# Transposed local probabilities and pooled value products of the later batches write to the bank ring of the first matrix product

## Chip, cores and metric

One core of a Trainium2 chip runs the whole program. The metric is the device time of one execution in microseconds, the median of three runs. A profile of one more execution gives the rows that are shown here.

## What is computed

The reference chains an attention and two feed-forward stages, all in fp32:

```
q, k, v: (4 batches, 8 heads, 576 positions, 64)
out_d   = softmax(mean4(q) @ mean4(k).T / 8) @ mean4(v)      # pooled: 144 x 144 per head
local   = softmax(q @ k.T / 8 where |i - j| < 4) @ v         # a band of 7
x       = (repeat4(out_d) + local) as (2304 tokens, 512)
y       = leaky_relu(x @ w_in, 0.01) @ w_out                 # 512 -> 2048 -> 512
out     = (h - tanh(h)) @ w_out2,   h = y @ w_in2            # 512 -> 2048 -> 512
```

## The kernel before

**Tokens and blocks.** Each batch is cut into five units of 116 positions (the last one shorter), 20 units in all. Four units make a block of 460 or 464 tokens, so there are five blocks, and each feed-forward stage goes through all five: blocks 0 to 4 of the first stage, then five of the second.

**The feed-forward.** For a block, `f` counts 16 slices of the hidden layer, and one turn of that loop is called a step here. In a step `gemm1` (line 390) makes the hidden slice in a tile `hp` with 12 matmuls, ScalarE applies the activation (line 506 in the first stage) and rounds it to `gh` (line 511), VectorE makes the remainder `gl` (line 512), and `gemm2` (line 401) adds the slice of two steps ago to four accumulators with another 12 matmuls. Block 0 also converts the first stage's weights on the way (lines 333 to 353, ScalarE and VectorE), and its steps need those weights.

**The attention.** A local unit goes through three stages: scores (line 260) and their softmax; four transposes of the probabilities (line 287), copied out by ScalarE (line 289); the value product (line 301), added to the pooled result by VectorE (line 311). A pooled item (one pair of heads of one batch) also has three: scores (line 166) and softmax (lines 174 to 184); transposes (line 194), copied out at line 197; the value product (line 202), copied out at line 206. The units and pooled items of block 1 are computed while the feed-forward of block 0 runs, and so on. At the end of each step `advance()` emits the next stage of each item in flight, the oldest first; at most three are in flight.

**The order.** A scheduler that runs when the program is built puts the instructions on the engines by the order in which they were emitted and by when it expects their inputs; the engines then run their queues in that order. A tile that shares a tag with others takes one of the tag's buffers.

**PSUM.** Eight banks: four for the accumulators (`acc0`, `acc2`), two for `px`, two for the ring `h`. While the first batch's attention runs, before the feed-forward, the accumulator banks serve as `pe` tiles. After that (`early["on"]` is False) every attention product of the later units and batches takes the one `px` buffer of two banks:

```
ps_h = ctx.enter_context(tc.tile_pool(name="ps_h", bufs=2, space=bass.MemoryType.PSUM))
hp = ps_h.tile([128, 512], F32, tag="h", name="hp")          # gemm1, one for each f
p = banks()[:, 0]                                            # line 199, pooled value product
p = banks()[:, 0]                                            # line 284, transposed local probabilities
```

So the ring `h` holds nothing but `hp` tiles from the first step on, and `px` goes round through six kinds of product.

Of the kernel before, what the change touches and what calls it, by code (L numbers as in the profile page):

```python
# [7 lines left out]
F32 = mybir.dt.float32  # L8
# [56 lines left out]
def tile_attention_moe(  # L65
# [19 lines left out]
    ps_h = ctx.enter_context(tc.tile_pool(name="ps_h", bufs=2, space=bass.MemoryType.PSUM))  # L85
# [24 lines left out]
    early = {"on": True, "n": 0}  # L110

    def banks(first=False):
        if early["on"]:
            early["n"] += first
            tag = EARLY_S[early["n"] % len(EARLY_S)] if first else EARLY_T
            if tag != "px":
                return ps_a.tile([128, 2, 512], F32, tag=tag, name="pe")
        return ps_x.tile([128, 2, 512], F32, tag="px", name="px")

    nat = {}  # L120

    def load_first():
# [37 lines left out]
    def emit_down(b, c):  # L160
        qs, vs = pooled[b][0][:, c], pooled[b][1][:, c]
        ps = banks(True)
        for ii in range(2):
            for par in range(2):
                r = slice(par * D, (par + 1) * D)
                nc.tensor.matmul(  # L166
                    out=ps[:HD, par, ii * SD:(ii + 1) * SD], lhsT=qs[r, 0, ii * HD:(ii + 1) * HD],
                    rhs=qs[r, 1, :], start=True, stop=True,
                )
        nm = sb.tile([HD, 2, 2], F32, tag="nm", name="nm", bufs=3)  # L170
        sm = sb.tile([HD, 2, 2], F32, tag="sm", name="sm", bufs=3)
        pr = sb.tile([HD, 2, 2, SD], F32, tag="pr", name="pr", bufs=PRB)
        pv = ps[:HD, :, :2 * SD].rearrange("p b (a j) -> p b a j", a=2)
        nc.vector.tensor_reduce(nm, pv, AX.X, ALU.max)
        nc.vector.tensor_scalar(out=nm, in0=nm, scalar1=-SCALE / 16.0, scalar2=None, op0=ALU.mult)
        for par in range(2):
            for ii in range(2):
                nc.scalar.activation(  # L178
                    out=pr[:, par, ii, :], in_=pv[:, par, ii, :], func=ACTF.Exp,
                    bias=nm[:, par, ii:ii + 1], scale=SCALE / 16.0, accum_out=sm[:, par, ii:ii + 1],  # L180
                )
        nc.vector.tensor_scalar(out=sm, in0=sm, scalar1=1e-9, scalar2=4.0, op0=ALU.add, op1=ALU.mult)
        nc.vector.reciprocal(out=sm, in_=sm)
        nc.vector.tensor_tensor(
            out=pr, in0=pr, in1=sm.unsqueeze(3).to_broadcast([HD, 2, 2, SD]), op=ALU.mult
        )
        yield
        pt = sb.tile([HD, 2, 2, SD], F32, tag="pt", name="pt", bufs=PTB)
        p = banks()
        for par in range(2):  # L190
            for jj in range(2):
                for ii in range(2):
                    o = jj * SD + ii * HD
                    nc.tensor.transpose(  # L194
                        p[:HD, par, o:o + HD], pr[:, par, ii, jj * HD:(jj + 1) * HD], id_sb[:HD, :HD]
                    )
        nc.scalar.copy(out=pt, in_=p[:HD, :, :2 * SD].rearrange("p b (a j) -> p b a j", a=2))
        yield
        p = banks()[:, 0]
        for jj in range(2):  # L200
            for par in range(2):
                nc.tensor.matmul(  # L202
                    out=p[par * D:(par + 1) * D, :SD], lhsT=vs[:, jj, par, :], rhs=pt[:, par, jj, :],
                    start=(jj == 0), stop=(jj == 1),
                )
        nc.scalar.copy(out=outd[b][:, c, :], in_=p[:, :SD])
        if b == 0:
            yield
            n = BLOCKS[0][1]
            dst = xf[0][:, c, :n].rearrange("p (i r) -> p i r", r=4)  # L210
            up = outd[0][:, c, :n // 4].unsqueeze(2).to_broadcast([128, n // 4, 4])
            nc.vector.tensor_tensor(out=dst, in0=dst, in1=up, op=ALU.add)
            split_x(xf[0], split0(), c, n)
# [20 lines left out]
    def emit_unit(i):  # L234
        b, u, n = UNITS[i]
        j = i // BU
        off = b * S + u * QB - BLOCKS[j][0]
        if i not in loaded:
            load_unit(i)
        q, kt, v = loaded.pop(i)  # L240

        def operands(r, c, k):
            if q is not None:
                return q[r, c, k], kt[r, c, k]
            t = nat[(k % 2) * 2 + k // 2]
            w = (2 * u + c) * CB
            return t[r, 0, HALO + w:HALO + w + KB], t[r, 1, w:w + KB]

        kind = 0 if u == 0 else (2 if u == NU - 1 else 1)
        p = banks(True)  # L250
        pv = p[:, :, :NC * KB].rearrange("p h (k x) -> p h k x", x=KB)
        for h in range(2):
            r = slice(h * D, (h + 1) * D)
            if i < U_PE:
                edge = band_sb[:, kind].unsqueeze(1).to_broadcast([128, NC, KB])
                nc.tensor.matmul(out=p[:, h, :NC * KB], lhsT=id_bf, rhs=edge, start=True, stop=False)
            for k in range(NC):
                for c in range(2):
                    lhs, rhs = operands(r, c, k)
                    nc.tensor.matmul(  # L260
                        out=pv[c * KB:(c + 1) * KB, h, k], lhsT=lhs, rhs=rhs,
                        start=i >= U_PE, stop=i >= U_PE or k == NC - 1,
                    )
        nm = sb.tile([128, 2 * NC], F32, tag="lnm", name="lnm", bufs=4)
        sm = sb.tile([128, 2 * NC], F32, tag="lsm", name="lsm", bufs=4)
        pr = slot("lpr", i).rearrange("p (h k x) -> p h k x", h=2, k=NC)
        nmv, smv = (t.rearrange("p (h k) -> p h k", h=2) for t in (nm, sm))

        def each(t):
            return t.unsqueeze(3).to_broadcast([128, 2, NC, KB])  # L270

        if i >= U_PE:
            edge = band_f[:, kind].unsqueeze(1).unsqueeze(1).to_broadcast([128, 2, NC, KB])
            nc.vector.tensor_tensor(out=pr, in0=pv, in1=edge, op=ALU.add)
            pv = pr
        nc.vector.tensor_reduce(nmv, pv, AX.X, ALU.max)
        nc.vector.tensor_tensor(out=pr, in0=pv, in1=each(nmv), op=ALU.subtract)
        nc.scalar.activation(out=pr, in_=pr, func=ACTF.Exp, scale=SCALE)
        nc.vector.tensor_reduce(smv, pr, AX.X, ALU.add)
        nc.vector.tensor_scalar(out=sm, in0=sm, scalar1=1e-9, scalar2=None, op0=ALU.add)  # L280
        nc.vector.reciprocal(out=sm, in_=sm)
        nc.vector.tensor_tensor(out=pr, in0=pr, in1=each(smv), op=ALU.mult)
        yield
        p = banks()[:, 0]
        prt = pr.rearrange("p h (f g) x -> p (h f) (g x)", g=2)
        for t in range(NC):
            nc.tensor.transpose(p[:, t * 128:(t + 1) * 128], prt[:, t], id_sb)  # L287
        ptf = slot("lpt", i)
        nc.scalar.copy(out=ptf, in_=p)
        pt = ptf.rearrange("p (h f c x) -> p h f c x", c=2, f=2, h=2)  # L290
        if BU <= i + NLD < len(UNITS):
            load_unit(i + NLD)
        yield
        p = banks().rearrange("p g (f x) -> p (g f) x", f=2)
        for c in range(2):
            m = min(CB, n - c * CB)
            for g in range(2):
                r = slice(g * KB, (g + 1) * KB)
                for f in range(2):
                    for h in range(2):  # L300
                        nc.tensor.matmul(  # L301
                            out=p[h * D:(h + 1) * D, g * 2 + f, c * CB:c * CB + m],
                            lhsT=v[r, c, f, h], rhs=pt[r, h, f, c, :m], start=True, stop=True,
                        )
        if j not in xf:
            xf[j] = sb.tile([128, NC, NMAX], F32, tag="xf", name="xf")
        if i < BU:
            nc.scalar.copy(out=xf[j][:, :, off:off + n], in_=p[:, :, :n])
            return
        up = outd[b][:, :, u * QB // 4:(u * QB + n) // 4]  # L310
        nc.vector.tensor_tensor(
            out=xf[j][:, :, off:off + n].rearrange("p c (i r) -> p c i r", r=4),
            in0=p[:, :, :n].rearrange("p c (i r) -> p c i r", r=4),
            in1=up.unsqueeze(3).to_broadcast([128, NC, n // 4, 4]), op=ALU.add,
        )
# [295 lines left out]
```

## Time and profile before

| what | us |
|---|---|
| median of 3 runs | 939.44 (937.93 to 940.49) |
| the profiled execution | 937.61 |
| its span, first to last instruction | 935.7 |
| around the span | 1.9 |

The profile names an instruction by engine, line, operation and tiles (`hp<-xh,w` writes `hp` and reads `xh` and `w`). PE is TensorE's matmuls and PEld its weight loads, DVE is VectorE, ACT is ScalarE, POOL is GpSimd. PEclk is the share of TensorE's full clock that was granted. A matmul's end is modelled, and pipelined matmuls overlap: their starts are the safer reading.

### The profile page before, as it was taken

To read this page: it belongs to the slowest core of one execution; us is meant where nothing else is said; L and a number is where in the kernel's file an instruction comes from. 1 tells how busy PE (TensorE), PEld (TensorE's weight loads), DVE (VectorE), ACT (ScalarE), POOL (GpSimd) and SP (SyncE) were. 2 spreads that over 40 slices of the span, in tenths; PEclk is the share of its full clock that TensorE was granted. 3 is DMA by queue.
4 is the path that set the end of the run, shared out by engine and by line. 5 is a ranking of instruction groups with operands and counts; after the bars stand their busy time and mean duration, and the time that the engine had idled before them with its cause. 6 is when DMAs were issued, how large, how long until landed. Compare 5 with 4: busy or idle time off the path is not lost.

```text
span 935.7 us, 13925 instructions
## 1 busy us (share of the span) xinstructions
PE 915.6 (98%) x5790; PEld 796.0 (85%) x5790; DVE 432.3 (46%) x779; ACT 354.2 (38%) x731; POOL 46.0 (5%) x76
## 2 busy tenths in 40 slices
PE   7889999999999999999999999999999999999997
PEld 6777788788887888888888888888888988888896
DVE  6989994444244414512366878322232223223222
ACT  2666654342344233222454645232232233224221
POOL 1011130013000100000000000000000000000000
PEclk9979999999999999999999999999999999999999
DMA  9996362146010202000466800010020010001001
GB/s 318 393 263 205 70 131 96 35 105 151 11 64 23 71 11 86 25 0 7 168 222 203 279 5 1 20 61 1 1 81 1 1 59 22 1 1 41 1 1 40
DMA packets 25790, 76.58 MB, mean 82 GB/s; under 512 B 3200, under 2 KB 10624, under 8 KB 25728
## 3 DMA queue, kind: packets, MB, share of 16 engines
q1 hardware_dynamic: 19008, 52.50, 15.8%
q0 software_dynamic: 6720, 23.21, 10.0%
q8 instruction: 45, 0.74, 0.3%
q14 instruction: 17, 0.14, 0.0%
HBM read 66.26 MB, written 9.44 MB: 81 GB/s over the span
## 4 chain that ended last, share of the span: by engine, by line
PE 91%; DMA 3%; ACT 2%; DVE 2%; issue 1%; SPq 0%; ACTq 0%; DVEq 0%
PE hp L390 43%; PE acc L401 42%; PE px L260 2%; DMA qk<-qk 1%; DMA v<-vd 1%; PE px L301 1%; PE px L287 1%; PE px L202 1%; PE px L166 1%; DMA out<-ev 1%; PE px L194 1%; DMA x2d<-ev 0%; ACT wm L333 0%; ACT w L352 0%; ACT pr L178 0%
## 5 line engine op out<-in xcount | busy, mean ns | idle before, releaser
L390 PE MATMUL hp<-xh,w 128*128 128x460 f32 (+1 forms) x1280 | 379.9, 377 | 4.3 <-ACT xh L368 2.2
L401 PE MATMUL acc<-gh,w 128*128 128x460 f32 (+1 forms) x1280 | 373.0, 372 | 0.0
L390 PEld LDWEIGHTS hp<-xh,w 128*128 128x128 f32 x1280 | 238.0, 189 | 35.6 <-issue 3.9
L401 PEld LDWEIGHTS acc<-gh,w 128*128 128x128 f32 x1280 | 240.0, 188 | 27.2 <-issue 0.2
L390 PE MATMUL hp<-xl,w 128*128 128x460 f32 (+1 forms) x640 | 239.6, 375 | 0.0
L401 PE MATMUL acc<-gl,w 128*128 128x460 f32 (+1 forms) x640 | 237.2, 371 | 0.0
L512 DVE TENSOR_TENSOR gl<-tg,gh 128x460 fp32r<-128x460 f32 (+1 forms) x160 | 101.8, 636 | 179.9 <-ACT gh L511 179.4
L509 DVE TENSOR_TENSOR tg<-hp,tg 128x460 f32<-128x460 f32 (+1 forms) x80 | 50.9, 637 | 196.7 <-ACT tg L508 196.7
L401 PEld LDWEIGHTS acc<-gl,w 128*128 128x128 f32 x640 | 120.2, 188 | 14.3 <-issue 0.2
L390 PEld LDWEIGHTS hp<-xl,w 128*128 128x128 f32 x640 | 120.7, 189 | 13.3 <-issue 0.4
L508 ACT ACTIVATE tg<-hp 128x460 f32<-128x460 f32 (+1 forms) x80 | 44.5, 556 | 184.3 <-PE hp L390 181.5
L511 ACT CAST gh<-tg 128x460 fp32r<-128x460 f32 (+1 forms) x160 | 92.3, 577 | 54.5 <-DVE tg L509 52.8
L506 ACT ACTIVATE tg<-hp 128x460 f32<-128x460 f32 (+1 forms) x80 | 44.4, 554 | 144.8 <-PE hp L390 144.7
L353 DVE TENSOR_TENSOR w<-wm,w 128x512 fp32r<-128x512 f32 x64 | 42.0, 687 | 8.2 <-ACT w L352 7.6
L333 ACT ACTIVATE wm<-raw 128x512 f32<-128x512 f32 x64 | 41.4, 672 | 7.5 <-DVE w L353 4.4
L345 DVE SCALAR_TENSOR_TENSOR wm<-raw,wm 128x512 uint32<-128x512 uint32 x64 | 43.4, 684 | 0.5
L340 DVE SCALAR_TENSOR_TENSOR wm<-raw,wm 128x512 int32<-128x512 int32 x64 | 43.3, 685 | 0.8
L352 ACT CAST w<-wm 128x512 fp32r<-128x512 f32 x64 | 36.9, 618 | 14.8 <-DVE wm L345 12.5
L534 ACT COPY ev<-acc 128x460 f32<-128x460 f32 (+1 forms) x38 | 19.8, 546 | 48.6 <-PE acc L401 31.5
L369 DVE TENSOR_TENSOR xl<-xf,xh 128x460 fp32r<-128x460 f32 (+1 forms) x40 | 24.4, 634 | 26.3 <-ACT xh L368 26.2
L368 ACT CAST xh<-xf 128x460 fp32r<-128x460 f32 (+1 forms) x40 | 22.0, 575 | 30.4 <-PE hp L390 27.7
L337 DVE TENSOR_SCALAR wm<-wm 128x512 int32<-128x512 int32 x64 | 26.7, 420 | 4.6 <-ACT wm L333 3.9
(75 smaller groups left out, 448.6 us busy)
## 6 DMA issues: line engine op xcount, KB each, us to landing
raw<-wts SPq DMA_DIRECT2D x64, 512.0 KB, 5.7
qs<-qkd POOLq DMA_DIRECT2D x12, 576.0 KB, 6.0
q<-qw POOLq DMA_DIRECT2D x16, 256.0 KB, 4.3
k<-kw POOLq DMA_DIRECT2D x16, 256.0 KB, 4.8
v<-vw POOLq DMA_DIRECT2D x16, 256.0 KB, 4.7
x2d<-ev SPq DMA_DIRECT2D x16, 230.0 KB, 2.1
xf<-x2d SPq DMA_DIRECT2D x4, 920.0 KB, 5.1
out<-ev SPq DMA_DIRECT2D x16, 230.0 KB, 2.9
```

The lines of the kernel that those rows point to most:

```text
L333: nc.scalar.activation(out=m, in_=st[:, :, 1].bitcast(F32), func=ACTF.Abs, scale=W_SCALE)
L340: nc.vector.scalar_tensor_tensor(out=m, in0=st[:, :, 1], scalar=-0x80000000, in1=m, op0=ALU.bitwise_and, op1=ALU.bitwise_or)
L345: nc.vector.scalar_tensor_tensor(out=m, in0=st[:, :, 0].bitcast(U32), scalar=29, in1=m, op0=ALU.logical_shift_right, op1=ALU.bitwise_or,)
L352: nc.scalar.copy(out=hi, in_=m)
L353: nc.vector.tensor_tensor(out=lo, in0=m, in1=hi.bitcast(F32), op=ALU.subtract)
L390: nc.tensor.matmul(out=hp[:, :n], lhsT=w[:, cs], rhs=r[:, c, :n], start=(c == 0 and i == 0), stop=(c == NC - 1 and i == 2),)
L401: nc.tensor.matmul(out=acc[m][:, :n], lhsT=w[:, cs], rhs=r[:, :n], start=(f == 0 and i == 0), stop=(f == NF - 1 and i == 2),)
L506: nc.scalar.activation(out=tg[:, :n], in_=hp[:, :n], func=ACTF.Prelu, alpha=0.01)
L508: nc.scalar.activation(out=tg[:, :n], in_=hp[:, :n], func=ACTF.Tanh)
L509: nc.vector.tensor_tensor(out=tg[:, :n], in0=hp[:, :n], in1=tg[:, :n], op=ALU.subtract)
L511: nc.scalar.copy(out=gh[:, :n], in_=tg[:, :n]),
L512: nc.vector.tensor_tensor(out=gl[:, :n], in0=tg[:, :n], in1=gh[:, :n].bitcast(F32), op=ALU.subtract),
```

## The change

Two of the six kinds of product leave `px`: the pooled value product (line 199) and the transposed local probabilities (line 284) take a tile of the ring `h` once the first batch's attention has been emitted. Before that point nothing changes, since `banks1` then returns what `banks()[:, 0]` did. No instruction is added or removed. The tiles that move are those of 12 pooled items (three later batches, four pairs of heads) and of 16 units (4 to 19).

```diff
+    def banks1():
+        if early["on"]:
+            return banks()[:, 0]
+        return ps_h.tile([128, 512], F32, tag="h", name="ph")
...
         yield
-        p = banks()[:, 0]
+        p = banks1()
         for jj in range(2):
...
         yield
-        p = banks()[:, 0]
+        p = banks1()
         prt = pr.rearrange("p h (f g) x -> p (h f) (g x)", g=2)
```

## Rows read from the trace of the kernel before

**Rows 1.** The page: busy time of the engines, and the group of line 506.

```profile
PE 915.6 (98%) x5790; PEld 796.0 (85%) x5790; DVE 432.3 (46%) x779; ACT 354.2 (38%) x731; POOL 46.0 (5%) x76
...
L506 ACT ACTIVATE tg<-hp 128x460 f32<-128x460 f32 (+1 forms) x80 | 44.4, 554 | 144.8 <-PE hp L390 144.7
```

**Rows 2.** Windows, all engines: blocks 0, 1, 3 and 4 of the first stage.

```profile
core 0: us, PE busy (x) PEld busy (x) DVE busy (x) ACT busy (x) POOL busy (x), PEclk, DMA share, GB/s
...
53.83:156.82 102.99, 102.74 (x726) 85.67 (x727) 89.04 (x173) 63.90 (x139) 17.31 (x25) 0.98 0.57 156
156.82:256.28 99.46, 99.42 (x754) 83.15 (x752) 37.29 (x72) 35.60 (x88) 13.12 (x20) 1.00 0.31 78
...
355.74:446.30 90.56, 90.39 (x658) 78.47 (x656) 29.43 (x52) 26.54 (x48) 3.23 (x6) 1.00 0.11 39
446.30:526.47 80.17, 80.17 (x385) 72.10 (x384) 50.97 (x89) 41.40 (x74) 0.00 (x0) 1.00 0.59 195
```

**Rows 3.** Windows, instructions on `px` alone: blocks 1, 3 and 0.

```profile
156.82:256.28 99.46, 17.77 (x368) 13.24 (x368) 8.30 (x12) 12.18 (x44) 1.00 0.31 78
...
355.74:446.30 90.56, 9.39 (x272) 7.43 (x272) 5.28 (x8) 2.35 (x4) 1.00 0.11 39
53.83:156.82 102.99, 18.88 (x342) 13.50 (x336) 11.00 (x16) 12.18 (x44) 0.98 0.57 156
```

**Rows 4.** Waits of PEld in block 1: total us, times, longest.

```profile
PEld px L301 <- issue: 1.3, 4, 0.3
PEld px L166 <- ACT pt L197: 1.0, 3, 0.3
PEld px L287 <- DVE xf L311: 0.7, 2, 0.4
...
PEld px L260 <- ACT lpt L289: 0.6, 2, 0.3
```

**Rows 5.** Timeline of the first batch's attention, 19 to 33 us: start, duration, instruction.

```profile
19.31 0.69 DVE L282 TENSOR_TENSOR lpr<-lpr,lsm 128x512 f32<-128x512 f32 x1
...
23.33 0.74 DVE L184 TENSOR_TENSOR pr<-pr,sm 72x576 f32<-72x576 f32 x1
...
27.25 0.71 PE L202 MATMUL pe<-pt,vs 72*64 72x144 f32 x8
...
28.48 0.66 PE L287 MATMUL pe<-id_sb,lpr 128*128 128x128 f32 x4
...
32.14 0.69 PE L194 MATMUL pe<-id_sb,pr 72*72 72x72 f32 x8 [0.42 <-ACT xf L308]
```

**Rows 6.** Timeline of PE in block 0, 70 to 140 us.

```profile
70.97 0.58 PE L390 MATMUL hp<-xh,w 128*128 128x464 f32 x2
...
73.28 0.60 PE L287 MATMUL px<-id_sb,lpr 128*128 128x128 f32 x4
...
74.65 0.71 PE L166 MATMUL px<-qs 64*72 64x144 f32 x8
...
97.34 0.37 PE L390 MATMUL hp<-xh,w 128*128 128x464 f32 x1
...
108.63 0.67 PE L194 MATMUL px<-id_sb,pr 72*72 72x72 f32 x8
...
114.10 0.71 PE L202 MATMUL px<-pt,vs 72*64 72x144 f32 x8
...
121.25 0.58 PE L390 MATMUL hp<-xh,w 128*128 128x464 f32 x2
...
137.79 0.63 PE L287 MATMUL px<-id_sb,lpr 128*128 128x128 f32 x4
```

**Rows 7.** Timeline of DVE in block 0, 44 to 158 us.

```profile
67.93 0.68 DVE L277 TENSOR_TENSOR lpr<-px,lnm 128x512 f32<-128x512 f32 x1
```

**Rows 8.** Windows, all engines: most of block 0.

```profile
65.00:145.00 80.00, 79.75 (x628) 65.37 (x627) 75.05 (x150) 51.20 (x116) 14.76 (x21) 1.00 0.59 157
```

**Rows 9.** Windows, all engines: two stretches about the feed-forward's first step.

```profile
54.00:56.00 2.00, 2.00 (x6) 1.72 (x7) 2.00 (x5) 0.88 (x2) 0.28 (x1) 0.50 0.99 299
...
62.00:64.00 2.00, 2.00 (x11) 1.79 (x10) 1.97 (x5) 1.74 (x4) 0.00 (x0) 1.00 1.06 267
```

**Rows 10.** Groups by line: the copy of a pooled value product.

```profile
L206 ACT COPY outd<-px 128x144 f32<-128x144 f32 x12 | 3.3, 279 | 9.8 <-PE px L202 9.8
```

## Prediction

> **What bounds the kernel now.** I read the page first: TensorE's matmuls are busy 98% of the span, no other engine half of it [rows 1]. So what counts is TensorE time, and a change of banks can alter it only where TensorE waits or where it switches between kinds of product. Next I cut the span at the blocks. A first-stage block that has no attention beside it (block 4) takes 80.17 us; blocks 1 and 3 take 99.46 and 90.56, and block 0 takes 102.99 [rows 2]. In block 1, TensorE is busy 99.42 of 99.46 us. Third, I asked for the instructions on `px` alone: 17.77 us of TensorE in block 1, 9.39 in block 3, 18.88 in block 0 [rows 3]. What a block takes beyond the bare block and its own attention is therefore 99.46 - 80.17 - 17.77 = 1.52 us in block 1 (block 2 has the same instructions and I take it as equal), 90.56 - 80.17 - 9.39 = 1.00 in block 3, and 102.99 - 80.17 - 18.88 = 3.94 in block 0. That remainder is all that waiting for `px`, and switching to and from it, can cost today.
>
> Block 0 is the odd one. From 65 to 145 us VectorE is busy 75.05 of 80 us and TensorE 79.75 [rows 8]: two engines are full at once, because the weights are converted there. In block 1 VectorE has 37.29 busy of 99.46 [rows 2]. So an attention chain that goes over VectorE is slow in block 0 and quick in the others.
>
> **The change, part by part.** No instruction goes or comes; 28 tiles move from `px` to `h`. Three things follow.
>
> *1. `px` goes round faster.* A product that had to wait until the copy of a transpose or of a pooled value product had emptied `px` no longer does. From below, this is worth almost nothing: in block 1 the weight loads of line 260 sit idle 0.3 us in each wait on that copy, those of line 287 0.7 in two waits, and line 301 sits idle the same 0.3 each time when it waits for nothing but issue [rows 4]. Only 0.1 us of a block's waits exceeds that. Line 166's waits on the pooled transposes (1.0 in three) stay, since both remain on `px`. From above, it is the whole remainder: 2 x 1.52 + 1.00 + 3.94 = 8.0 us. In between lies what the scheduler can do with the freedom: a pooled value product and the next pooled transposes, which were kept apart by the copy between them, can stand side by side, so that TensorE leaves the feed-forward once and not twice. I take a quarter of the remainder, **-2.0 us**, nearer to the waits that are seen than to the whole.
>
> The Trainium skill (Perfetto Trace Analysis, Optimization Strategy) says that a gap that repeats on the engine that should be full can mean that there is too little PSUM for the next tile. By that rule the whole 8.0 us would come back. The gaps are there, but the same 0.3 us stands before a product that waits for no bank [rows 4], so I don't follow it all the way.
>
> *2. The ring `h` gets more tiles, and hands them out in the order of the program.* Whether a shared buffer goes to whoever is ready or to whoever is next in the program, the first batch's attention shows. There lines 194, 202, 287 and 301 share one buffer. The probabilities of unit 0 were done at 20.00 (19.31 + 0.69) and those of the second pooled item at 24.07 (23.33 + 0.74), but their transposes ran at 28.48 and 32.14, behind the pooled value product of the first item at 27.25, which precedes them in the program [rows 5]. So a later tile waits for its turn even if its data are there. If the two-buffer ring behaves so too, the emission order counts. In block 0 `advance()` puts the moved tiles between the `hp` tiles so (T: transposes of a unit, V: value product of a pooled item): hp2 T4 hp3 hp4 V0 hp5 V1 hp6 V2 hp7 V3 T5 hp8 T6 hp9 T7 hp10 hp11. With two buffers a tile needs the one two places before it to be empty. Hence hp4 needs T4, hp8 needs V3 and hp11 needs T7; the others need the `hp` before them, that is its activation of 0.55 us [rows 1], which gemm2 covers with 12 matmuls: half of a bare step, 80.17 / 32 = 2.5 us [rows 2].
>
> In blocks 1 to 3 the attention keeps up with the program, because VectorE is idle most of the time, and the moved tiles are emptied before their successor asks: nothing lost there.
>
> In block 0 it lags. T4 ran at 73.28, but hp4 had begun at 70.97; V3 ran at 114.10, but hp8 had begun at 97.34; T7 ran at 137.79, but hp11 had begun at 121.25 [rows 6]. All three first products would have to come later than now. Behind hp8 on TensorE's queue wait all later first products and, with them, their second products.
>
> - hp4: from 70.97 it moves behind T4 (73.28 + 0.60, and its copy). The next second product, 2.5 us, is ready to stand in front: nothing lost.
> - hp8, from above: if V3 stayed at 114.10, its copy (0.28 us) [rows 10] would end near 115.1, 17.8 us after hp8's present start. In that time TensorE could do the second products of steps 6 and 7 (5.0 us) and the attention that it does now between 97.34 and 115 (three value products, two transposes, one pooled score product at some 0.7 us, unit 5's scores at 1.6: about 5.9). 6.9 us would be idle.
> - hp8, from below: V3 itself comes earlier, since the first pooled score product now waits (until 74.65) for T4 to leave `px`. Afterwards it could start when line 277 has read the scores of unit 4, at 68.61 (67.93 + 0.68) [rows 7]. All of the 6.0 us passed on would leave 0.9 us idle. And V3 now came after unit 5's scores, 5.5 us after its own transposes (108.63 to 114.10) [rows 6]; if it follows them within 2 us, nothing is idle. But the chain of the pooled items goes over VectorE, which has no room, and two pieces of conversion will stand in front of each link. I pass on 4.3 us of the 6.0, and take **+2.6 us**.
> - hp9 and hp10: TensorE has then used up its stock of second products, and each of these two waits for the activation before it, 0.55 us and some 0.2 of signalling; part is filled by attention. **+0.8 us** (0 to 3).
> - hp11: T7 depends on unit 7's scores, which no longer wait for the transposes of unit 6 to be copied. I expect it some 13 us sooner, at about 124, and there is stock again: nothing, at worst 2.
>
> *3. Copies and loads.* The copies of lines 206 and 289 are the same and their readers too; q, k, v loads are issued by the same lines and wait for the same products. Nothing.
>
> **The sum.** -2.0 + 2.6 + 0.8 = +1.4 us on the profiled execution: 937.6 + 1.4 = 939.0. Its time stands 1.8 below the median of the runs, so the median would be 939.44 + 1.4 = **940.8 us**. Here 0.3% is 2.8 us, and less than that a measurement of this kernel can't tell from no change.
>
> **Rivals.**
> - *The ring doesn't bind; only `px` gains.* If the scheduler gives the two-buffer ring to whichever tile is ready, or V3 comes in time, part 1 alone is left, and more of it: 3 us of the 8.0. For it: the waits named above do exist [rows 4]. Against it: rows 5. 936.4, at the edge of the faster side, which is reached from 2.8 us upward.
> - *The ring binds hard in block 0.* V3 stays late because VectorE decides when the softmaxes finish [rows 8]: 6.9 us idle before hp8, 1.5 behind it, 2.0 gained: +6.4, 945.8. It decides from the point at which V3 comes less than about 3 us sooner than now.
> - *The clock falls.* While TensorE was idle before the feed-forward its granted clock fell to 0.50, the 1.2 GHz level, and stayed there into the first step: 6 matmuls touched 2 us against 11 at 1.00 [rows 9]. If the waits before hp8 bring that on, some 10 us at the lower level, about what it lasted there, cost 5 us on top: 945.8. Against it: waits of 2 us beside 0.7 us products are not idleness. The Trainium skill (TensorE: Matmul & The Clock Gate, "A second HAM failure mode: psum-queue depth-cycling") describes a kernel whose cycling through PSUM banks left enough small gaps for its clock to go back and forth; in this kernel the clock is at 1.00 through block 1 with six kinds of product on one buffer [rows 2].
> - *Nothing moves.* The gaps at the switches are issue and not banks [rows 4], and TensorE finds enough other work in block 0: 939.4. This lies inside the forecast's own range.
>
> **Chances.** The forecast with its near neighbours, within 2.8 us either way: 0.43. Ring doesn't bind: 0.27, nearly all of it faster by over 0.3%, 0.24. Ring binds hard: 0.25. Clock: 0.05. So faster 0.24, same 0.46, slower 0.30. The range: from the whole-hearted first rival (a gain of 4 us of the 8.0, 935.4) to the hard ring with the upper ends of hp9 to hp11 (6.9 + 3 - 2.0 = +7.9, 947.3); about 1 in 10 is left on each side.
>
> **What the new profile would show.** Right: the transposes of line 287 and the products of line 202 write a tile `ph`; the pooled chain in block 0 begins near 69 and its last value product comes at 104 to 107; hp8 begins behind it and not at 97; several second products stand together before hp8; TensorE idles 2 to 4 us in block 0; blocks 1 and 2 are each about 0.5 us shorter. Wrong: if hp8 begins near 97 with V3 unfinished, the ring isn't bound by the program's order, and the first rival holds. If TensorE has over 5 us idle before hp8, the hard ring holds. If blocks 1 to 3 get longer, a first product waits for a moved tile where I expect none.

## Result and profile after

The change makes the kernel slower. The median is 952.48 us (948.06 to 954.44, six runs), against 939.3 us for the kernel before on the same chip; the ratio is 1.0131, with a 95% interval of 1.0114 to 1.0148. The forecast was 940.8 us with a range up to 947.3. The profiled execution took 948.06 us (span 946.2) against 937.61 (935.7).

Line numbers are five higher than before (`gemm1` is line 395, `gemm2` 406, the transposes T line 292, the value product V line 207). The first two lines are of the page after the change, and answer to [rows 1].

```profile
PE 918.0 (97%) x5790; PEld 802.1 (85%) x5790; DVE 432.3 (46%) x779; ACT 354.4 (37%) x731; POOL 46.0 (5%) x76
...
L511 ACT ACTIVATE tg<-hp 128x460 f32<-128x460 f32 (+1 forms) x80 | 44.4, 555 | 150.5 <-PE hp L395 149.6
```

Windows after the change, all engines: blocks 0, 1, 3 and 4, the counterpart of [rows 2].

```profile
core 0: us, PE busy (x) PEld busy (x) DVE busy (x) ACT busy (x) POOL busy (x), PEclk, DMA share, GB/s
53.68:168.07 114.39, 105.30 (x727) 88.16 (x727) 89.53 (x173) 64.87 (x139) 17.34 (x25) 0.95 0.50 140
168.07:267.67 99.60, 98.90 (x754) 84.04 (x753) 37.13 (x72) 35.37 (x88) 13.11 (x20) 1.00 0.31 78
...
367.29:458.43 91.14, 90.25 (x658) 78.98 (x657) 29.35 (x52) 26.07 (x48) 3.22 (x6) 1.00 0.11 39
458.43:538.60 80.17, 80.17 (x386) 72.09 (x384) 50.98 (x89) 41.41 (x74) 0.00 (x0) 1.00 0.59 195
```

Read the lengths first. Block 0 went from 102.99 to 114.39 us, block 1 from 99.46 to 99.60, block 3 from 90.56 to 91.14, and block 4 is the same. Block 2 went from 99.46 to 99.62. So the loss is made in block 0. With blocks 1 to 3 (+0.9) it is 12.3; a start 0.15 earlier and two blocks of the second stage, shorter by 0.60 and 1.08, take it to the 10.45 us between the two profiled executions.

Then split block 0. TensorE's idle time is 114.39 - 105.30 = 9.09 us, where it was 102.99 - 102.74 = 0.25: +8.84. Its busy time rose by 105.30 - 102.74 = 2.56 us for the same products. The two make up the 11.40.

Waits of PE after the change in block 0 (total us, times, longest) name what ended the idle time.

```profile
PE ph L207 <- DMA vs<-vd: 4.6, 1, 4.6
PE ph L292 <- DVE lpr L287: 3.8, 3, 2.1
PE hp L395 <- ACT xh L373: 2.2, 1, 2.2
PE acc L406 <- ACT gh L516: 0.6, 1, 0.6
```

The 2.2 us at line 395 lie ahead of the block's first matmul, and the kernel before has them too. The other 9.0 us are the idle time: 4.6 for a load of pooled v, 3.8 in three waits of T for VectorE, 0.6 for a `gh`. No wait is for a bank.

The timeline of PE in block 0, the counterpart of [rows 6], shows what stood behind each moved tile.

```profile
68.62 0.71 PE L171 MATMUL px<-qs 64*72 64x144 f32 x8
...
72.76 0.65 PE L292 MATMUL ph<-id_sb,lpr 128*128 128x128 f32 x4 [1.12 <-DVE lpr L287]
73.17 0.67 PE L395 MATMUL hp<-xh,w 128*128 128x464 f32 x2
...
82.23 0.58 PE L406 MATMUL acc<-gh,w 128*128 128x464 f32 x2
82.75 0.71 PE L171 MATMUL px<-qs 64*72 64x144 f32 x8
88.06 1.15 PE L207 MATMUL ph<-pt,vs 72*64 72x144 f32 x8 [4.60 <-DMA vs<-vd]
89.14 1.14 PE L395 MATMUL hp<-xh,w 128*128 128x464 f32 x2
...
92.90 0.37 PE L406 MATMUL acc<-gl,w 128*128 128x464 f32 x1
...
97.02 0.71 PE L207 MATMUL ph<-pt,vs 72*64 72x144 f32 x8
97.66 0.69 PE L395 MATMUL hp<-xh,w 128*128 128x464 f32 x2
...
104.49 0.71 PE L207 MATMUL ph<-pt,vs 72*64 72x144 f32 x8
105.13 0.68 PE L395 MATMUL hp<-xh,w 128*128 128x464 f32 x2
...
113.14 0.71 PE L207 MATMUL ph<-pt,vs 72*64 72x144 f32 x8
...
119.18 1.11 PE L292 MATMUL ph<-id_sb,lpr 128*128 128x128 f32 x4 [2.09 <-DVE lpr L287]
119.95 1.12 PE L395 MATMUL hp<-xh,w 128*128 128x464 f32 x2
...
136.49 0.66 PE L292 MATMUL ph<-id_sb,lpr 128*128 128x128 f32 x4 [0.55 <-DVE lpr L287]
136.90 0.67 PE L395 MATMUL hp<-xh,w 128*128 128x464 f32 x2
```

At lines 292, 207 and 395 these are, from the top, T4 and hp3, V0 and hp5, V1 and hp6, V2 and hp7, V3, T5 and hp8, T7 and hp10. Each first product starts right behind the moved tile that precedes it in the program. V3 came at 113.14, no sooner than the 114.10 of before, and hp8, which had begun at 97.34, began at 119.95.

That this is not a wait for an empty bank can be seen at hp5. Going round in two banks with V0 ahead of it, hp5 writes the bank that hp4 used, and hp4's activation is in the timeline of ACT:

```profile
79.37 0.56 ACT L511 ACTIVATE tg<-hp 128x464 f32<-128x464 f32 x1
...
89.25 0.28 ACT L211 COPY outd<-ph 128x144 f32<-128x144 f32 x1 [6.64 <-PE ph L207]
89.43 0.62 ACT L357 CAST w<-wm 128x512 fp32r<-128x512 f32 x1
```

The bank was empty at 79.93 and hp5 began at 89.14, before V0's copy had even started. It stood behind V0 on TensorE's queue. The Trainium skill (PSUM — Partial Sum Buffer, "Engine vs sequencer instructions") says that matmuls start and complete in program order; the trace agrees, with hp5 1.08 us behind V0 and 9.2 us behind the emptying of its bank.

More than hp5 stood behind V0. Two matmuls of the second product that belongs to hp4 ran at 82.23, and the other ten came only at 92.90, behind hp5. They lacked no input, since VectorE had finished its `gl` at 81.49 + 0.63 = 82.12:

```profile
81.49 0.63 DVE L517 TENSOR_TENSOR gl<-tg,gh 128x464 fp32r<-128x464 f32 x1
```

At about 0.21 us each they could have filled some 2 of the 4.6 idle microseconds. TensorE took its queue in the order that was fixed when the program was built, and did not pick what was ready.

The wait spread: V0's copy stood first on ScalarE's queue, which was idle for 6.64 us with casts of the weights behind it, and VectorE in its turn waited 4.48 us for such a cast.

### The profile page after: what moved, and what is told of

Same layout as the page of the kernel before. It is cut to its first block, busy times and chain, and to the rows that moved or that the text cites. A ratio compares the mean times of both kernels' runs of the same rounds, so it can differ in the third digit from the quotient of the medians.

```text
span 946.2 us, 13913 instructions
## 1 busy us (share of the span) xinstructions
PE 918.0 (97%) x5790; PEld 802.1 (85%) x5790; DVE 432.3 (46%) x779; ACT 354.4 (37%) x731; POOL 46.0 (5%) x76
## 4 chain that ended last, share of the span: by engine, by line
PE 87%; DMA 7%; DVE 3%; ACT 1%; issue 1%; POOL 0%; SPq 0%; POOLq 0%; ACTq 0%
PE hp L395 41%; PE acc L406 39%; DMA vs<-vd 3%; DMA qs<-qkd 2%; PE px L265 2%; DMA qk<-qk 1%; PE ph L292 1%; PE warm L468 1%; PE ph L207 1%; PE px L199 1%; DVE lpr L287 1%; DVE lsm L284 1%; PE px L306 1%; PE px L171 1%; ACT tg L511 0%
```

## Experiments

All ratios are to the kernel before on the same chip.

**Where, and which tiles.** Three runs keep part of the change: T alone, V alone (the other takes `banks()[:, 0]` as before), and both but only from block 1 on.

```diff
 # e3: both, from block 1 on
+    later = []
     def banks1():
-        if early["on"]:
+        if not later:
             return banks()[:, 0]
...
+        if idx == 1:
+            later.append(idx)
```

> Only the transposed local probabilities (T) go to the ring; the pooled value products (V) stay on px. Theory (order): a first product isn't issued before the moved tile that precedes it in the program, so the loss is the idle time before moved tiles that are late, and the lower clock after it. T5, T6 and T7 then come when they did in the kernel before (about 118, 128, 138 us), the first product of step 8 not before T5, and TensorE runs out of other work: block 0 some 108 to 112 us, 945 to 949 in all, idle only before transposes. Rival (load): only the wait of V0 for the pooled v counts; T costs nothing: 939 to 941. Rival (capacity): what costs is that a tile too many shares two banks; half the tiles, half the loss: 945 to 946, with waits spread before first products.

> Only the pooled value products (V) go to the ring; the transposes of the units stay on px. Order: 4 to 5 us idle before V0, which waits for the last load of the pooled v, a lower clock after it, no idle time before a transpose: block 0 some 108 to 111 us, 945 to 949. Load: the whole loss, 950 to 953. Capacity: under half of the loss (12 tiles of 28), about 944 to 945, no wait longer than an activation.

> Both kinds go to the ring, but only from block 1 on; in block 0 they stay on px. Order: block 0 is 103 us again, blocks 1 to 3 are 0.1 to 0.6 us longer each as in the changed kernel: 939.5 to 941. If instead part of the loss lies in blocks 1 to 3 or later, which one profile of the changed kernel would not have shown: over 942.

T alone: 946.13 us, 1.0076 (1.0052 to 1.0101), block 0 109.70. V alone: 947.77 us, 1.0093 (1.0063 to 1.0123), block 0 109.13. Both from block 1 on: 938.1 us, 0.9993 (0.9981 to 1.0005), which is below the 939.5 to 941 expected, although blocks 1 to 3 are longer as expected (99.59, 99.63 and 91.14). The windows of block 0 and block 1 of this last kernel:

```profile
54.87:158.05 103.18, 103.02 (x727) 85.79 (x728) 89.03 (x173) 63.88 (x139) 17.32 (x25) 0.98 0.55 154
158.05:257.64 99.59, 98.89 (x753) 84.05 (x752) 37.19 (x72) 35.33 (x88) 13.06 (x20) 1.00 0.30 78
```

Without the moved tiles, block 0 is back at its old length. Either kind alone lengthens it by over 6 us, as order foretold, so neither is harmless there. The two don't add up (6.7 and 6.1, together 11.4). The waits are not all where they were expected. With T alone, T waits 2.5 us for VectorE, but attention products on `px` wait 2.1 us too, for that buffer. With V alone, V0 waits 2.1 us for its load and not 4 to 5; the rest is a wait of pooled transposes for their softmax (1.8) and one of a second product for a `gh` (1.3). In blocks 1 and 2, T alone gave 99.88 and 99.84, V alone 99.40 and 99.33: it is T that makes them longer.

**Do more tiles use up the ring?** This kernel has the old places for T and V, and at each of them an extra tile of the ring: one matmul of 32 columns whose inputs are always ready, and its copy on ScalarE.

```diff
 # kernel before
+    def extra():
+        if not early["on"]:
+            p = ps_h.tile([128, 512], F32, tag="h", name="extra")
+            nc.tensor.matmul(out=p[:, :32], lhsT=id_bf, rhs=id_bf[:, :32], start=True, stop=True)
+            t = sb.tile([128, 32], F32, tag="extra", name="extra_sb", bufs=2)
+            nc.scalar.copy(out=t, in_=p[:, :32])
...
+        extra()
         p = banks()[:, 0]
```

> The kernel before, with 28 further tiles in the ring at the places in the program where the change puts its own: each gets one matmul of 32 columns on inputs that are always there and a ScalarE copy of 32 columns. As many tiles share two banks as in the changed kernel, but none is late. Order: only their own work, some 0.2 to 0.3 us of TensorE each, 2 us in block 0: 940 to 946, no idle time over 0.5 us in block 0. Capacity: block 0 as in the changed kernel, over 110 us, 948 to 955.

942.92 us, 1.0027 (1.0005 to 1.0048), block 0:

```profile
54.65:158.49 103.84, 103.38 (x735) 85.34 (x735) 89.15 (x173) 64.88 (x147) 17.38 (x25) 0.98 0.56 153
```

Block 0 is 0.85 us longer than before, and TensorE is idle in it for 0.46 us, against 0.25. Eight more tiles in block 0 do little as long as their inputs are there. The Trainium skill (Perfetto Trace Analysis, "Optimization Strategy") says that a repeated gap on the engine that should be full can mean too little PSUM for the next tile. Here it did not: the gaps of the changed kernel don't come back when the same number of tiles with ready inputs goes round in the same two banks.

**The load of pooled v.** The longest wait, before V0, is for the last of four accumulating loads of pooled v. First their order in the program was interleaved with that of the pooled q and k; then `vs` got a second buffer and its loads were placed right behind the first load of `qs`.

```diff
 # e7
...
-        vs = sb.tile([HD, NC, 2, 2, D], F32, tag="vs", name="vs")
-        nc.gpsimd.dma_start(out=qs, in_=qkd[b, 0])
-        nc.gpsimd.dma_start(out=vs, in_=vd[b, 0])
+        vs = sb.tile([HD, NC, 2, 2, D], F32, tag="vs", name="vs", bufs=2)
+        first_q = nc.gpsimd.dma_start(out=qs, in_=qkd[b, 0])
+        with behind([first_q]):
+            nc.gpsimd.dma_start(out=vs, in_=vd[b, 0])
+            for r in range(1, 4):
+                nc.gpsimd.dma_start(out=vs, in_=vd[b, r], accum_op=ALU.add)
...
-        for r in range(1, 4):
-            nc.gpsimd.dma_start(out=vs, in_=vd[b, r], accum_op=ALU.add)
```

> The changed kernel with the loads of pooled v put between those of pooled q and k, so that the last of them lands before V0 is due. Order: the 4.6 us before V0 go, and with them the lower clock behind it; the waits before T4, T5 and T7 stay: block 0 some 107 to 110 us, 942 to 947. Load: all of the loss goes: 939 to 941. Capacity: the loads don't matter: 950 to 953.

> The changed kernel with a second buffer for pooled v and its loads put into the queue behind the first load of pooled q and k, so that they are over long before V0. Order: the idle time before V0 (4.6 us) and the lower clock after it go; waits before T4, T5 and T7 stay: block 0 some 106 to 110 us, 942 to 948. Load: the whole loss goes, 937 to 941. Capacity: no change, 949 to 953.

The interleaved order moved no load: the first was issued at 58.11 us and the last at 85.08 (83.40 with the change alone), so this run says nothing of the load; as a near repeat of the change it gave 950.63 us, 1.0122 (1.0099 to 1.0144), and block 0 took 116.95 us in its profiled execution. With the second buffer: 944.57 us, 1.0062 (1.0039 to 1.0085). Its last load went out at 62.34, V0 ran at 85.04 without a wait, and block 0:

```profile
54.67:163.71 109.04, 104.33 (x726) 87.29 (x727) 89.53 (x173) 64.83 (x139) 14.88 (x22) 0.96 0.50 143
```

So the late load, with what followed from it, accounts for 114.39 - 109.04 = 5.35 us of block 0 (4.38 of idle time and 0.97 of busy time), and 6.05 are left that it does not explain.

**Start the chain later.** Is the chain only late in absolute time, so that a later start of the moved stages hides it? In this run block 0 emits no attention before its fourth step; the control does the same to the kernel before.

```diff
-            if moe == 0:
+            if moe == 0 and (j or f >= 3):
                 advance()
```

> The changed kernel, but in block 0 the attention of the next block is first advanced in step 3 instead of step 0, so that every moved tile stands three steps later in the program, near the time at which it is really ready. Tiles, banks and loads are the same. Order: no first product waits for a moved tile for more than 1 to 2 us; block 0 some 103 to 106 us, 938 to 943. Capacity (too many tiles for two banks): no change, 949 to 953. Load: V0 waits no longer, the same as order.

> Control: the kernel before with the same later start. Nothing stands in the ring but hp tiles, so all theories expect no change that can be measured: 937 to 941.

949.21 us, 1.0093 (1.0061 to 1.0124), block 0 114.04: no help, a miss for what was expected. The control gave 938.51, 0.9988 (0.9969 to 1.0008), and its block 0 102.84. The timeline of PE in the changed kernel with the late start:

```profile
105.03 0.71 PE L207 MATMUL ph<-pt,vs 72*64 72x144 f32 x8
105.67 0.69 PE L395 MATMUL hp<-xh,w 128*128 128x464 f32 x2
...
112.53 0.71 PE L207 MATMUL ph<-pt,vs 72*64 72x144 f32 x8
113.17 0.69 PE L395 MATMUL hp<-xh,w 128*128 128x464 f32 x2
```

The same lockstep, V0 17 us later. The load did not shift, so V0 no longer waits for it, and yet block 0 is as long: T waits 3.0 us for VectorE, second products wait 3.3 us for `gh` and `gl`, and TensorE's busy time is 107.71 us, 2.41 more than with the change, at a mean granted clock of 0.93. A T and the softmax that feeds it shift together, so the distance between a tile's inputs and its turn stays what it was. Lateness had to be read relative to the tile's own inputs.

**Leave the chain where it is, and move only V and T later.** Here the stages that feed V and T are emitted as in the changed kernel, and only V and T of block 0 come three steps (three `hp` tiles) later. So that the next ones can start meanwhile, up to six units and items are in flight in block 0 in place of three, and a unit's loads are issued before its T waits.

```diff
+LATER = 3
...
         yield                       # pooled item, before V
+        for _ in range(LATER if b == 1 else 0):
+            yield
         p = banks1()
...
         yield                       # unit, before T
+        if i // BU == 1:
+            load_unit(i + NLD)
+            for _ in range(LATER):
+                yield
         p = banks1()
...
-        if not order or len(flight) >= (FLIGHT0 if early["on"] else FLIGHT):
+        if not order or len(flight) >= (FLIGHT0 if early["on"] else FLIGHT + LATER if limit[0] < 2 else FLIGHT):
```

The second run adds the second `vs` buffer of above.

> The kernel with the change, but in block 0 alone the moved stages (V of batch 1, T of units 4 to 7) stand three steps later in the program, while the scores and probabilities that feed them stand where they stood. Strict program order: each first product still goes behind the tile just before it, but that tile's inputs are now ready three steps (about 7.5 us) ahead of its place, so the lockstep of block 0 is gone but for V0, whose load of pooled v is as late as before: block 0 is 103 to 107 us instead of 114.4, the whole 938 to 943 us. If what lengthens block 0 is the stages' own work in these banks and not the wait for their inputs, the place in the program changes nothing: block 0 stays at 112 us or more and the whole is 948 to 953 us.

> The edit of the run before together with a second buffer for pooled v, whose loads then start early. Strict program order: with neither the chain nor the load late at its place, block 0 is 103 to 104 us and the whole is 938 to 941 us, no different from the kernel before. Own work: block 0 stays at 109 us as with the second buffer alone, and the whole is 943 to 947 us.

944.33 us, 1.0043 (1.0025 to 1.0061), block 0 108.42; with the second buffer 946.04, 1.0063 (1.0042 to 1.0084), block 0 110.57. Both miss what was expected by strict order. But up to the eleventh first product (hp10) the first of them is as quick as the kernel before: 60.5 us from the start of block 0, against 59.3 before and 83.2 with the change. What follows begins with one wait of PE, at the scores of unit 7 (line 268 here):

```profile
118.42 0.73 PE L268 MATMUL px<-k,q 64*64 64x64 f32 x16 [2.69 <-DMA k<-kw]
```

With six units and items in flight, the scores of units 5 to 7 came within 11 us (19 before), and the k of unit 7 had been issued at 111.22 only, behind the next batch's pooled loads. The second buffer made that wait 4.2 us. Two runs take it away: a third buffer for the local q, k and v (`NLD = 3`), or four in flight (`FLIGHT + 1` in place of `FLIGHT + LATER`).

> The kernel with the moved stages three steps later in block 0, and a third buffer for the local q, k and v tiles. In the run with the later stages alone, block 0 took as long to its eleventh first product as before the change (60.5 us against 59.3), and then lost the rest in one wait, 2.72 us for the k of unit 7 whose load stood behind the pooled loads, and in what followed it. The third buffer lets that k load a unit earlier. Strict program order: block 0 is 103 to 105 us, the whole 938 to 941.5 us, within 0.3 per cent of before. If the stages' own work in these banks costs the time, block 0 stays above 107 us and the whole at 942 to 946 us.

> The same later stages, without the third buffer, but with four units and items in flight in block 0 instead of six, so that the scores of units 5 to 7 don't follow so closely on each other and unit 7's k is not wanted so soon. Strict program order: block 0 is 103 to 105.5 us, the whole 938 to 942 us. Own work: block 0 above 107 us, the whole 942 to 946 us.

Third buffer: 941.34 us, 1.0012 (0.9991 to 1.0034), block 0 102.58 (its stage began 3 us later, at 56.97, and block 5 took 84.4). Four in flight: 938.29 us, 0.9978 (0.9962 to 0.9994). Both are in the range that order gave for the whole. Windows of block 0 of this last one, and its timeline of PE (V is line 210 here, `gemm1` 402, T 299):

```profile
55.06:157.76 102.70, 102.41 (x726) 85.97 (x727) 88.62 (x173) 63.69 (x139) 18.67 (x25) 0.98 0.56 155
```

```profile
97.91 0.71 PE L210 MATMUL ph<-pt,vs 72*64 72x144 f32 x8
98.55 0.68 PE L402 MATMUL hp<-xh,w 128*128 128x464 f32 x2
...
133.10 0.71 PE L210 MATMUL ph<-pt,vs 72*64 72x144 f32 x8
133.74 0.66 PE L299 MATMUL ph<-id_sb,lpr 128*128 128x128 f32 x4
```

All 28 tiles are still on the ring, each first product still stands right behind its tile, V3 even runs 20 us later than in the changed kernel, and block 0 is 102.70 us. The tiles and the banks are those of the change, and so is the place of a first product behind each; with the inputs there at a tile's turn, nothing of the 11.4 us is left. This run also has four in flight and earlier unit loads, and the kernel before was not run with these two alone; but its block 0 has only 0.25 us of idle time that they could have saved.

**Which move is worth keeping.** Two kernels move V alone: from block 1 on, and everywhere but three steps later in block 0 (with four in flight).

> Only V on the ring, and only from block 1 on; the transposes stay in the pair of scores. With V alone on the ring blocks 1 and 2 were 0.06 and 0.13 us shorter than before, so by strict program order this is 0.1 to 0.4 us below the kernel before, 938.5 to 939.5 us, which five rounds can hardly tell from no change. If the shorter blocks were chance, it is within 0.1 per cent on either side.

> Only V on the ring, three steps later in block 0 with four in flight there; the transposes stay in the pair of scores. By strict program order block 0 is 102.5 to 103.5 us (with both, later, it was 102.70) and blocks 1 to 3 are 99.34, 99.34 and 90.57 us as with V alone, 1.1 us less than with both: 936.8 to 938.5 us, 0.1 to 0.3 per cent below the kernel before. If the transposes' place mattered for block 0, or the shorter blocks are given back, it is 939 to 941 us.

From block 1 on: 938.66 us, 0.9984 (0.9967 to 1.0002), not told from no change. Everywhere, later in block 0: 936.77 us, 0.9976 (0.9961 to 0.9990), the quickest of all, though its ratio is not told from the 0.9978 of both kinds with four in flight. Its windows of blocks 0 and 1:

```profile
53.43:156.19 102.76, 102.55 (x727) 85.91 (x727) 88.20 (x173) 63.86 (x139) 17.16 (x25) 0.98 0.57 158
156.19:255.53 99.34, 99.31 (x753) 83.36 (x752) 37.18 (x72) 35.48 (x88) 13.12 (x20) 1.00 0.31 78
```

Only 0.5 us of it can be read from blocks 0 to 3 (0.23, 0.12 and 0.12). The rest of the 1.9 us between the profiled spans is a start 0.4 earlier and a block 7 that is 1.1 shorter; that block took 80.17 us in every profiled execution but those of the kernel before and of the extra tiles, so nothing ties it to this edit. That moving V gains anything is not shown.

## Why the prediction was wrong

- **The step that failed** is "With two buffers a tile needs the one two places before it to be empty", and the list drawn from it (hp4, hp8 and hp11 bound, the rest free). The program order was read rightly from [rows 5], but it binds more tightly: a first product goes behind the tile *just* before it, on TensorE's queue, whether its own bank is empty or not. Right behind a moved tile stood hp3, hp5, hp6, hp7, hp8, hp9 and hp10. "hp4 ... nothing lost" became 1.1 us idle before T4, with hp3 behind it. The second products that were to fill the waits were used up before T4 and T5, and before V0 ten matmuls of one were ready but stood behind hp5 on the queue. Whether the hand-out of the ring or the times that the scheduler expects keep a first product behind the tile before it, no run separates.
- **hp8, hp9 and hp10 (+2.6 and +0.8)** stand for what was 8.84 us of idle time. No row shows the 0.2 us of signalling in the second; the waits measured behind hp8 are 0.59 us for a `gh` and 0.55 before T7. V3 was to come at 104 to 107 and came at 113.14: the chain begins at 68.62, as the prediction said, but of the 6 us that it began sooner 1.3 were left at V0 (88.06 against 89.32).
- **"Copies and loads ... Nothing"** was the second failure. The last load of pooled v was issued at 83.40, against 84.44 before, so it was no later than it had been; before, TensorE did other products until V0 at 89.32. In the ring V0 stands ahead of hp5, and the load became a 4.6 us wait, 5.35 us of block 0 with what followed (the run with the second buffer).
- **Part 1 (-2.0).** In block 1 TensorE's busy time did fall by 99.42 - 98.90 = 0.52 us, the forecast's 0.5, and a pooled value product and the next pooled transposes do stand side by side (200.54 and 201.18), as it said. But its idle time rose from 0.04 to 0.70. The one group of waits of PE in block 1 is this:

```profile
PE ph L292 <- DVE lpr L287: 0.7, 2, 0.4
```

  T waits for VectorE there, and the runs with one kind alone show that it comes with T: V alone has blocks 1 and 2 at 99.40 and 99.33. That T has this wait because the first product behind it keeps it in place is argued; no run separates it. "Nothing lost there", of blocks 1 to 3, was wrong by 0.1 to 0.6 us each.
- **The rivals.** "The ring binds hard" (945.8) had the right condition: V3 came 0.96 us sooner, less than its 3. Its idle time, 6.9 + 1.5, is near the 8.84 measured, though not before hp8 but in front of V0, T4, T5 and T7. It still fell short of the result, since it took 2.0 off for part 1 and left the clock out. That its 945.8 came nearest is in part luck. "The clock falls", held at 0.05, came true beside it: 2.56 us of busy time, against the 5 that it was priced at. It called TensorE idle before the feed-forward; from 48 to 54 us, at 0.50, it was busy for 2.7 of 6 us. "The ring doesn't bind" is refuted by the windows of block 0 and the run from block 1 on. That capacity was the cause is refuted by the extra tiles, and by the run with four in flight, where the moved tiles themselves go round in the two banks.

The median is 4.4 us above the profiled execution. The five other executions had spans of 947.7 to 952.5 us at a mean granted clock of 0.984 to 0.987, against 946.2 at 0.990. Half a hundredth of clock over 950 us is about 9.5 us at the half level instead of the full one, which by this estimate loses some 4.8 us. So the clock can be most of the difference, but it is not all: 947.7 and 952.2 us both came at 0.987. Where those executions lost the time stays open, since only one of them left a trace. The near repeat with interleaved loads points to block 0: its span is 949.8 us, and of the 3.7 us above 946.2 block 0 has 2.56, 1.9 of it busy time.

## What to carry to other kernels

When a tile moves to a ring that the bounding engine also writes, look at what stands just behind it in the program, and ask when the tile's inputs are ready compared with its turn. A spare bank would not have helped hp5, whose bank was empty, since it stood behind the tile on the same queue (a third bank was not tried); emitting the late tile a few steps later did help, provided that the work which feeds it stays in place and that the loads of whatever now runs sooner are early enough. A transfer or a softmax that was hidden only because its reader could slip back has to be priced again when the reader is pinned.

## What was not expected of the hardware

TensorE's granted clock fell after two idle stretches in mid-run, of 4.6 and 2.1 us. Windows of 2 us after the change, around V0 and around T5 (PE's busy time is the second number, PEclk the one after POOL's):

```profile
86.00:88.00 2.00, 0.00 (x0) 0.00 (x0) 0.00 (x0) 0.00 (x0) 0.00 (x0) 1.00 0.84 213
88.00:90.00 2.00, 1.94 (x10) 1.51 (x11) 0.00 (x0) 0.75 (x3) 0.00 (x0) 0.55 0.03 12
90.00:92.00 2.00, 2.00 (x7) 1.72 (x7) 1.10 (x4) 2.00 (x11) 0.00 (x0) 0.60 0.00 0
92.00:94.00 2.00, 2.00 (x11) 1.77 (x11) 1.97 (x4) 1.45 (x4) 0.00 (x0) 1.00 0.00 0
...
118.00:120.00 2.00, 0.82 (x5) 0.82 (x5) 2.00 (x5) 0.55 (x1) 0.74 (x2) 0.73 0.77 129
120.00:122.00 2.00, 2.00 (x7) 1.75 (x6) 1.52 (x4) 1.11 (x2) 0.00 (x0) 0.50 1.02 263
```

While TensorE was idle the granted clock still read 1.00; it fell when work came back, to 0.55 and 0.60, near the 1.2 GHz level, and 7 matmuls touched 2 us where 11 do at 1.00. The 1.1 us of idle time before T4 brought no such fall: the 2 us windows from 70 to 78 us all read 1.00. In the run with the late start, two waits of 1.5 and 1.2 us close to each other, before 96.72 and 99.07, were followed by 0.50 from 100 to 104 us. So a wait can cost more than itself: in the run with the second buffer, without the 4.6 us before V0, block 0 is 5.35 us shorter, 0.97 of it busy time.
